# Re-ordering the input loads of a fused attention and FFN kernel over three DMA queues, with a new order of the small steps in its second block

## The chip, the cores and the metric

The kernel runs on one core of one Trainium2 chip. The metric is the device time of one execution in microseconds (us); smaller is better. Before the change the median of three executions was 339.74 us (338.42 to 339.96).

## The reference, cut to what matters

Eight batches of linear attention give `x`, and `x` goes through a gated feed-forward network (FFN). Batches, heads, tokens and head width are 8, 8, 576, 64; the FFN is 512 to 1536 to 512.

```python
def phi(x, c, s):                       # c, s: cosine and sine of the token's position
    r = np.maximum(x, 0.0)
    return np.concatenate([r * c, r * s], axis=-1)
q_p = phi(q, cos_w, sin_w);  k_p = phi(k, cos_w, sin_w)
kv  = np.einsum('bhsf,bhsd->bhfd', k_p, v);   z = np.sum(k_p, axis=2)
num = np.einsum('bhsf,bhfd->bhsd', q_p, kv)
den = np.einsum('bhsf,bhf->bhs', q_p, z)[..., None] + 1e-06
x   = num / den                          # then tokens x (heads*width) = 4608 x 512

xn  = x / np.sqrt(np.mean(x * x, -1, keepdims=True) + 1e-06) * rms_g
g   = xn @ w_gate;  out = (g / (1 + np.exp(-g)) * (xn @ w_val)) @ w_out
```

## The kernel before

The FFN runs in blocks of 512 tokens, one per batch. Block b has 16 steps. Steps 0 to 11 are gate and value matmuls (`psG`, `psV`), and steps 12 to 15 are output matmuls (`psC`). Between them sits the attention of batch b+1: the feature maps `k_phi` and `q_phi` (half on VectorE, half on ScalarE), the cast of v, the transposes of q, the k-z-v matmuls (`kv` and `z` of the reference), the numerator and denominator matmuls (`nd_pe`, below "numerator/denominator"), the norm, and the transpose of x that the next block multiplies. In block 0 the transposes run on TensorE; from block 1 on they are DMA transposes issued by SyncE. The last 64 tokens of a batch (the "tail") are handled in pairs of batches and make a ninth block.

A load is issued by an engine into a queue of DMA work, and lands some time later. All loads of q, k and v are issued by SyncE, in the order in which they are needed. The three weights are loaded by the GpSimd queue, which casts them to bf16 on the way.

```python
nc.scalar.preload_act_table(AF.Silu)
V, A, G = nc.vector, nc.scalar, nc.gpsimd
LOW, HIGH = (0, 4), (4, 8)                       # heads
# ... load_main, load_tail and load_pair call nc.sync.dma_start ...
load_main("k", k, 0, LOW, two)
load_main("k", k, 0, HIGH, two)
load_tail("k", k, 0)
load_pair("q", 0, 0)                             # two of the four token columns of q
load_main("v", v, 0, LOW)
first["v"] = load_tail("v", v, 0)
load_main("v", v, 0, (4, 6))
load_main("v", v, 0, (6, 8))
load_pair("q", 0, 1)
# ... the opening: attention of batch 0, and a third of block 0's first steps ...

def first_loads_of_1():
    d = load_main("k", k, 1, bufs=two)
    tc.add_manual_dep(d.ins, weight_dmas[4].ins.name, SYNC_DEP, reason="after the weights")
    load_tail("k", k, 1)
    gate = load_main("q", q, 1)
    load_main("v", v, 1, LOW)
    load_main("v", v, 1, HIGH)
    load_tail("v", v, 1)
    for i in range(4):
        d = nc.gpsimd.dma_start(out=wo[:, 3*i : 3*i+3, :], in_=moe_w_out[...])
        wo_dmas.append(d)
        if i == 0:
            tc.add_manual_dep(d.ins, gate.ins.name, SYNC_DEP, reason="after batch 1")
```

The last two lines are a gate: GpSimd does not start loading `w_out` until q of batch 1 has landed.

The order of the small steps in block 1 (`late` is true there, `nb` is batch 2; each step's DMA transposes follow its feature map):

```python
kb, kn = (b, (c + 1) // 2) if late else ...      # k_phi of batch 2, piece c
qn = 5 + (c * 3) // 5 if late else c             # q_phi and its DMA transpose, c = 0..4
vb, vn = (b, 3) if late else ...                 # cast of v
kz, nds = (7, (8, 10, 12, 13)) if late else ...  # k-z-v; numerator/denominator 0..3
# x_norm and the DMA transpose of x follow one step after each of nds
...
at(1, 2 + bb, "post", q_phi, ..., bb, 4, ...)    # tails of q, batches 0 and 1, steps 2 and 3
at(1, 2 + bb, "post", q_tr_dma, bb, 4)
at(1, 3, "post", load_tail, "q", q, 2)
at(1, 6, "pe", nd_pe, 1, 4, psA)                 # tail of the first pair of batches
at(1, 7, "post", x_tr_dma, 1, 4)
```

## Time and profile before

The profiled execution took 340.11 us, its span is 338.3 us and the mean granted TensorE clock is 0.988.

| landmark (profiled execution) | us |
|---|---|
| first FFN matmul | 19.91 |
| block 1 starts (first 256-column `psG` group) | 60.20 |
| step 2 of block 1 | 64.80 |
| block 2 starts | 101.98 |
| its second `psG` group | 105.17 |
| end of the span | 338.3 |

From the page of the kernel before, these are the busy times (share of the span, instruction count), the load of the DMA engines in 40 slices of 8.5 us (tenths) and the chain that ended last, by engine.

```profile
PE 322.0 (95%) x2157; PEld 163.9 (48%) x2193; DVE 181.5 (54%) x372; ACT 169.4 (50%) x327; POOL 38.1 (11%) x83
...
DMA  8999999948793966797769676967552220020014
...
PE 87%; DMA 4%; issue 2%; ACT 2%; DVE 2%; SPq 2%; POOL 0%; ACTq 0%; DVEq 0%; POOLq 0%
```

TensorE (PE) is the bound, but over the first eight slices, some 68 us, the DMA engines are full too.

The next lines are from the timeline of TensorE of the kernel before. The columns are start, length, engine, source line, operation, output from inputs, shape, count; the bracket gives the idle time before it and what ended it.

```profile
19.91 0.38 PE L511 MATMUL psG<-xnT,wg 128*128 128x128 bf16 x4 [0.30 <-DVE xnT L273]
...
44.63 0.39 PE L423 MATMUL psC<-wo,hT 128*128 128x512 bf16 x1 [0.59 <-DMA wo<-in_moe_w_out_dram]
...
74.14 0.60 PE L321 MATMUL psA<-kvzs,qtT 128*64 128x65 bf16 x15 [2.12 <-DMA qtT<-qp]
74.68 1.46 PE L403 MATMUL psG<-xnT,wg 128*128 128x512 bf16 x3
...
101.98 1.89 PE L403 MATMUL psG<-xnT,wg 128*128 128x512 bf16 x4 [2.54 <-DMA xnT<-xn]
...
105.17 1.03 PE L403 MATMUL psG<-xnT,wg 128*128 128x512 bf16 x4
```

TensorE stands still twice, in block 1 (until 74.14) and at its end (until 101.98), and works at half rate afterwards. A group of four 512-column matmuls takes 1.03 us in the last line, but 1.89 us just after the second wait. Both waits cost about 3.6 to 4 us each with that tail.

GpSimd's own waits in the same kernel show the gate at work:

```profile
POOL wo L601 <- DMA rq<-in_q_dram: 12.7, 1, 12.7
```

GpSimd waited 12.7 us, once, for q of batch 1 before it issued the load of `w_out`. GpSimd is no bottleneck, so this wait costs little by itself: TensorE's 0.59 us for `w_out` at 44.63.

### The profile page before, as it was taken

Reading aid. Unit: us, or ns where it says so; the run is one execution under the profiler, and the core shown is the slowest. Engines: PE = TensorE matmul, PEld = TensorE weight load, DVE = VectorE, ACT = ScalarE, POOL = GpSimd, SP = SyncE. Lnnn points to the kernel's source line nnn. Section 1 sums busy time; section 2 is a strip of 40 time slices with the busy share of each in tenths; the row PEclk is TensorE's granted clock in tenths of the full one; section 3 lists DMA queues with packets and bytes.
Section 4 is the critical chain, followed back from the end, with each engine's and each line's share of the span. In section 5 each row is a group of like instructions: output and inputs, shape, how many; then the busy total and the mean of one; then the engine's idle time right before and its main releaser. Section 6 shows DMA issues by size and latency. Waiting matters only on the chain.

```text
span 338.3 us, 5906 instructions
## 1 busy us (share of the span) xinstructions
PE 322.0 (95%) x2157; PEld 163.9 (48%) x2193; DVE 181.5 (54%) x372; ACT 169.4 (50%) x327; POOL 38.1 (11%) x83
## 2 busy tenths in 40 slices
PE   8889999879979999999999999999999999999994
PEld 3568455535433544454445444544454444444441
DVE  4675747575843576557536864685467323204410
ACT  5655844756454546554655465546645233223321
POOL 3520301101120012001100120011001100000000
PEclk9999999989997999999999999999999999999999
DMA  8999999948793966797769676967552220020014
GB/s 230 267 208 265 274 179 278 336 109 166 183 238 86 228 179 177 180 222 184 201 160 221 171 217 158 211 177 215 144 79 46 85 72 1 2 105 19 2 31 94
DMA packets 94957, 54.14 MB, mean 160 GB/s; under 512 B 59984, under 2 KB 90192, under 8 KB 94928
## 3 DMA queue, kind: packets, MB, share of 16 engines
q1 hardware_dynamic: 90160, 49.04, 57.6%
q0 software_dynamic: 4768, 4.72, 8.5%
q8 instruction: 17, 0.28, 0.4%
q14 instruction: 12, 0.10, 0.1%
HBM read 38.01 MB, written 9.44 MB: 140 GB/s over the span
## 4 chain that ended last, share of the span: by engine, by line
PE 87%; DMA 4%; issue 2%; ACT 2%; DVE 2%; SPq 2%; POOL 0%; ACTq 0%; DVEq 0%; POOLq 0%
PE psG L403 26%; PE psV L403 26%; PE psC L423 23%; PE psA L299 3%; PE psA L314 2%; DMA rv<-in_v_dram 2%; PE psG L423 1%; DMA xnT<-xn 1%; PE psO L511 1%; PE psG L511 1%; SPq L85 1%; PE psV L511 1%; DMA qtT<-qp 1%; SPq L76 1%; ACT scr L352 1%
## 5 line engine op out<-in xcount | busy, mean ns | idle before, releaser
L418 DVE TENSOR_TENSOR hT<-psV,sg 128x512 bf16<-128x512 f32 x102 | 70.3, 689 | 105.4 <-PE psV L403 78.8
L412 ACT ACTIVATE sg<-psG 128x512 f32<-128x512 f32 x102 | 60.6, 594 | 72.1 <-PE psG L403 67.0
L403 PE MATMUL psG<-xnT,wg 128*128 128x512 bf16 (+1 forms) x353 | 92.3, 379 | 4.5 <-DMA xnT<-xn 2.5
L403 PE MATMUL psV<-xnT,wv 128*128 128x512 bf16 (+1 forms) x364 | 93.3, 378 | 0.6 <-issue 0.2
L423 PE MATMUL psC<-wo,hT 128*128 128x512 bf16 x394 | 90.8, 379 | 1.2 <-DMA wo<-in_moe_w_out_dram 0.6
L403 PEld LDWEIGHTS <-wv 128*128 128x128 bf16 x416 | 41.1, 99 | 48.7 <-issue 2.2
L423 PEld LDWEIGHTS <-hT 128*128 128x128 bf16 x432 | 41.3, 98 | 48.3 <-DMA wo<-in_moe_w_out_dram 0.8
L403 PEld LDWEIGHTS <-wg 128*128 128x128 bf16 x416 | 38.9, 98 | 45.4 <-issue 3.0
L357 POOL TENSOR_TENSOR rs<-ms,mhalf 128x1 f32<-128x1 f32 x36 | 20.2, 562 | 206.0 <-ACT scr L352 206.0
L271 ACT COPY osb<-psC 128x512 f32<-128x512 f32 x33 | 19.4, 587 | 46.8 <-PE psC L423 46.8
L352 ACT ACTIVATE scr<-xt 128x513 bf16<-128x513 f32 x36 | 22.9, 636 | 24.8 <-DVE xt L340 23.9
L364 DVE SCALAR_TENSOR_TENSOR xn<-xt,rs,gb 128x512 bf16<-128x512 f32 x36 | 27.3, 760 | 14.1 <-POOL rs L357 13.9
L340 DVE TENSOR_TENSOR xt<-psA,rec 128x512 f32<-128x512 f32 x35 | 24.2, 691 | 1.2
L212 ACT ACTIVATE qp<-rq,tab 128x512 bf16<-128x512 f32 x32 | 22.2, 713 | 2.3 <-DMA rq<-in_q_dram 2.3
L212 ACT ACTIVATE kpm<-rk,tab 128x512 bf16<-128x512 f32 (+1 forms) x34 | 21.2, 675 | 2.5 <-DMA rk<-in_k_dram 2.4
L214 DVE TENSOR_SCALAR kpm<-rk,tab 128x512 bf16<-128x512 f32 (+1 forms) x38 | 15.2, 451 | 3.3 <-DMA rk<-in_k_dram 3.3
L314 PEld LDWEIGHTS <-qpT 128*128 128x128 bf16 x256 | 12.3, 98 | 8.0 <-issue 1.4
L214 DVE TENSOR_SCALAR qp<-rq,tab 128x512 bf16<-128x512 f32 x32 | 15.4, 493 | 0.6 <-DMA rq<-in_q_dram 0.6
L443 PE MATMUL psG<-warm 128*128 128x512 bf16 x47 | 13.8, 439 | 1.2 <-DVE fidx L149 1.2
L314 PE MATMUL psA<-kvzs,qpT 128*128 128x65 bf16 x248 | 13.0, 194 | 0.6 <-DVE xt L340 0.3
L403 PE MATMUL psG<-xnt_tail,wg 128*128 128x512 bf16 x48 | 12.3, 379 | 0.1
L403 PE MATMUL psV<-xnt_tail,wv 128*128 128x512 bf16 x47 | 12.1, 379 | 0.0
(82 smaller groups left out, 191.4 us busy)
## 6 DMA issues: line engine op xcount, KB each, us to landing
out_dram<-osb SPq DMA_DIRECT2D x32, 256.0 KB, 2.9
rv<-in_v_dram SPq DMA_DIRECT2D x22, 256.0 KB, 3.3
rk<-in_k_dram SPq DMA_DIRECT2D x20, 256.0 KB, 3.6
rq<-in_q_dram SPq DMA_DIRECT2D x20, 256.0 KB, 3.1
rk<-in_k_dram SPq DMA_DIRECT2D x2, 1024.0 KB, 7.0
rq<-in_q_dram SPq DMA_DIRECT2D x2, 1024.0 KB, 9.0
rv<-in_v_dram SPq DMA_DIRECT2D x3, 512.0 KB, 9.2
wo<-in_moe_w_out_dram POOLq DMA_DIRECT2D x4, 384.0 KB, 7.3
```

The lines of the kernel that those rows point to most:

```text
L212: nc.scalar.activation(out=out_ap, in_=in_ap, func=AF.Relu, scale=scale)
L214: eng.tensor_scalar(out=out_ap, in0=in_ap, scalar1=scale, scalar2=0.0, op0=ALU.mult, op1=ALU.max)
L271: nc.scalar.copy(out=o, in_=i)
L314: nc.tensor.matmul(o[:, g, i, :], lhsT=qpT[(b, 0)][:, h, j * P : (j + 1) * P], rhs=kvzs[b][:, g, i * E : (i + 1) * E], start=True, stop=True,)
L340: nc.vector.tensor_tensor(out=xt[:, 0:DM].rearrange("p (b h d) -> p b h d", b=2, d=D), in0=o[:, :, :, 0:D], in1=rec[:, :, :].unsqueeze(3). ...
L352: nc.scalar.activation(out=scr[:, :], in_=xt[:, 0 : DM + 1], func=AF.Square, scale=1.0 / math.sqrt(DM), accum_out=ms[:, :],)
L357: nc.gpsimd.tensor_tensor(out=rs[:, :], in0=ms[:, :], in1=mhalf[:, :], op=ALU.pow)
L364: nc.vector.scalar_tensor_tensor(out=xn[:, :], in0=x_of[(b, j)][:, 0:DM], scalar=rs_of[(b, j)][:, :], in1=gb[:, :], op0=ALU.mult, op1=ALU. ...
L403: nc.tensor.matmul(pst[bank][:, cols[0] : cols[1]], lhsT=w[:, t, n * P : (n + 1) * P], rhs=x[:, t, cols[0] : cols[1]], start=(t == 0), sto ...
L412: nc.scalar.activation(out=sg[:, :], in_=psG[bank][:, :], func=AF.Silu)
L418: nc.vector.tensor_tensor(out=hTs[blk][:, n, :], in0=psV[bank][:, :], in1=sg[:, :], op=ALU.mult)
L423: nc.tensor.matmul(bank, lhsT=hTs[blk][:, n, j * P : (j + 1) * P], rhs=wo[:, n, :], start=(n == 0), stop=(n == NNT - 1),)
```

## The change

It has four parts, named (a) to (d) as in the prediction:

- (a) The opening loads are split over SyncE's and ScalarE's queues, so that they are issued sooner. The load of ScalarE's activation table moves behind ScalarE's issues. Also, the first k-z-v uses single banks of PSUM (the memory into which TensorE writes), so that one half can be evicted while the other is computed.
- (b) v of batch 1 goes to the GpSimd queue, and the gate on `w_out` goes.
- (c) The tail of the first pair moves from step 6 of block 1 to step 14, to end the first wait. The rest of batch 2's attention moves up to one step earlier.
- (d) With that, the last transpose of x comes one step earlier, to end the second wait.

```diff
 first = {}
+load_pair("q", 0, 0, A)                 # A: ScalarE's queue
 load_main("k", k, 0, LOW, two)
+load_main("v", v, 0, LOW, queue=A)
 load_main("k", k, 0, HIGH, two)
+first["v"] = load_tail("v", v, 0, A)
 load_tail("k", k, 0)
-load_pair("q", 0, 0)
-load_main("v", v, 0, LOW)
-first["v"] = load_tail("v", v, 0)
+load_main("v", v, 0, (6, 8), queue=A)
 load_main("v", v, 0, (4, 6))
-load_main("v", v, 0, (6, 8))
 load_pair("q", 0, 1)
+nc.scalar.preload_act_table(AF.Silu)    # was the first instruction
 # ... cut: kvzs as one tile per bank, kvz_half in psG[1] and psV[1], more buffers ...
 x_norm(0, 1)
+load_main("v", v, 1, LOW, queue=G)      # G: GpSimd's queue
+load_main("v", v, 1, HIGH, queue=G)
+load_tail("v", v, 1, G)
 # ...
-gate = load_main("q", q, 1)
-load_main("v", v, 1, LOW)
-load_main("v", v, 1, HIGH)
-load_tail("v", v, 1)
+load_main("q", q, 1)
 # ... in the loop over the four pieces of w_out:
-    if i == 0:
-        tc.add_manual_dep(d.ins, gate.ins.name, SYNC_DEP, reason="after batch 1")
 # ... block 1:
-qn = 5 + (c * 3) // 5 if late else c
+qn = 4 + (c * 3) // 5 if late else c
-kz, nds = (7, (8, 10, 12, 13)) if late else (4, (5, 7, 9, 11))
+kz, nds = (6, (7, 9, 11, 12)) if late else (4, (5, 7, 9, 11))
-at(1, 6, "pe", nd_pe, 1, 4, psA)        # and its post, norm and transpose at 6 and 7
+at(1, 14, "pe", nd_pe, 1, 4, psA)       # now at 14 and 15
```

More of the change, by code (lines that the diff above doesn't have):

```diff
@@ L61 @@
     psO = ps_open.tile([P, 2, 512], FP32, name="psO")
-    nc.scalar.preload_act_table(AF.Silu)
     V, A, G = nc.vector, nc.scalar, nc.gpsimd
@@ L69, with load_main @@
     raw = {}
-    def load_main(which, src, b, heads=(0, 8), bufs=one):
+    def load_main(which, src, b, heads=(0, 8), bufs=one, queue=nc.sync):
         key = (which, b)
@@ L75, in load_main @@
         h0, h1 = heads
-        return nc.sync.dma_start(
+        return queue.dma_start(
             out=raw[key][:, h0:h1, :],
@@ L79, in load_main, with load_tail @@
         )
-    def load_tail(which, src, b):
+    def load_tail(which, src, b, queue=nc.sync):
         t = two.tile([P, 4, D], FP32, name=f"r{which}t", tag=f"r{which}t")
@@ L84, in load_tail @@
         for g in range(2):
-            d = nc.sync.dma_start(
+            d = queue.dma_start(
                 out=t[64 * g : 64 * g + 64, :, :],
@@ L104, in load, with load_pair @@
         last_load[(which, b)] = load_tail(which, src_of[which], b)
-    def load_pair(which, b, jj):
+    def load_pair(which, b, jj, queue=nc.sync):
         key = (which, b)
@@ L111, in load_pair @@
         view = src_of[which][b, :, 0:512, :].rearrange("h (p j) d -> p h j d", j=4)
-        return nc.sync.dma_start(
+        return queue.dma_start(
             out=raw[key][:, :, jj * 2 * D : (jj + 1) * 2 * D],
@@ L245, in q_dst @@
         if (b, c // 4) not in qpT:
-            qpT[(b, c // 4)] = two.tile(
+            qpT[(b, c // 4)] = (two if c < 4 else four).tile(
                 [P, H, 512] if c < 4 else [P, 4, P], BF16,
@@ L303, in kvz_evac, with kvz_half, kvz_half_evac @@
     def kvz_evac(eng, b, pst, bank):
-        if b not in kvzs:
-            kvzs[b] = two.tile([P, 2, 4 * E], BF16, name="kvzs", tag="kvzs")
-        copy(eng, kvzs[b][:, bank, :], pst[:, bank, 0 : 4 * E])
+        kvzs[(b, bank)] = three.tile([P, 4 * E], BF16, name="kvzs", tag=f"kvzs{bank}")
+        copy(eng, kvzs[(b, bank)][:, :], pst[:, bank, 0 : 4 * E])
+    def kvz_half(b, view, heads):
+        o = view[:, 0, 0 : 4 * E].rearrange("p (h e) -> p h e", e=E)
+        for h in heads:
+            for c in range(5):
+                lhsT = kp_main[b][:, c, h, :] if c < 4 else kpt[b % 2][:, h % 4, :]
+                rhs = vvm[b % 2][:, c, h, :] if c < 4 else vvt[b % 2][:, h, :]
+                nc.tensor.matmul(
+                    o[:, h % 4, :], lhsT=lhsT, rhs=rhs, start=(c == 0), stop=(c == 4)
+                )
+    def kvz_half_evac(eng, b, view, bank):
+        kvzs[(b, bank)] = three.tile([P, 4 * E], BF16, name="kvzs", tag=f"kvzs{bank}")
+        copy(eng, kvzs[(b, bank)][:, :], view[:, 0, 0 : 4 * E])
     def nd_pe(b, j, pst):
@@ L315, in nd_pe @@
                     o[:, g, i, :], lhsT=qpT[(b, 0)][:, h, j * P : (j + 1) * P],
-                    rhs=kvzs[b][:, g, i * E : (i + 1) * E], start=True, stop=True,
+                    rhs=kvzs[(b, g)][:, i * E : (i + 1) * E], start=True, stop=True,
                 )
@@ L323, in nd_pe @@
                         lhsT=qpT[(bb, 1)][:, i, 64 * g : 64 * g + 64],
-                        rhs=kvzs[bb][:, g, i * E : (i + 1) * E], start=True, stop=True,
+                        rhs=kvzs[(bb, g)][:, i * E : (i + 1) * E], start=True, stop=True,
                     )
@@ L477 @@
     filler(2, idle)
-    kvz_pe(0, psA, range(0, 4))
+    half_view = {
+        g: t[:, :].rearrange("p (b c) -> p b c", b=1) for g, t in ((0, psG[1]), (1, psV[1]))
+    }
+    kvz_half(0, half_view[0], range(0, 4))
     filler(1, idle)
@@ L482 @@
     v_cast(A, 0, (7, 8))
-    kvz_evac(A, 0, psA, 0)
-    kvz_pe(0, psA, range(4, 6))
+    kvz_half(0, half_view[1], range(4, 6))
     filler(1, idle)
-    kvz_pe(0, psA, range(6, 8))
+    kvz_half(0, half_view[1], range(6, 8))
     filler(2, idle)
-    kvz_evac(V, 0, psA, 1)
+    kvz_half_evac(A, 0, half_view[0], 0)
+    kvz_half_evac(V, 0, half_view[1], 1)
     for c in (2, 3):
@@ L738 @@
     at(1, 3, "post", load_tail, "q", q, 2)
-    at(1, 6, "pe", nd_pe, 1, 4, psA)
-    at(1, 6, "pre", nd_post, 1, 4, psA)
-    at(1, 6, "post", x_sq, 1, 4)
-    at(1, 7, "post", x_norm, 1, 4)
-    at(1, 7, "post", x_tr_dma, 1, 4)
+    at(1, 14, "pe", nd_pe, 1, 4, psA)
+    at(1, 14, "pre", nd_post, 1, 4, psA)
+    at(1, 14, "post", x_sq, 1, 4)
+    at(1, 15, "post", x_norm, 1, 4)
+    at(1, 15, "post", x_tr_dma, 1, 4)
     for blk in range(1, 9):
```

## The prediction

> **What bounds the kernel now.** The profile page has PE busy 95% of 338.3 us; the chain of waits is PE for 87%. Outside a saturated middle, the chain leaves PE in four places.
> 1. Opening: the chain runs SyncE's load issues, the v load (lands 12.77), ACT cast, k-z-v, numerator/denominator from 15.10, first FFN matmul at 19.91.
> 2. About 43.6 to 45.1: transposes and a wait for w_out; PE idle 0.59 us.
> 3. Block 1, step 6: PE waits 2.12 us at 72 to 74.14 for the transposed q tails (L321). The next eight 512-column matmuls take 3.2 us instead of 1.73 (cold clock): about 3.6 us in all.
> 4. End of block 1: PE waits 2.54 us (to 101.98) for the last x transpose of batch 2, and is cold again: about 4.0 us.
>
> **What changes.**
> (a) Opening. Five load issues move from SyncE to ACT, ahead of the table load (1.28 us). I expect this to lose. The Trainium skill ("DMA: Bandwidth & Descriptors", Queues, rings and completion order) says all queues share 16 engines, which go round-robin by packet; this trace agrees on saturation: the DMA row reads 9 from about 2.3 us on. So bytes do not come faster, only in another order: q (512-byte rows) now shares with k. In the instruction order ACT's fifth issue (v, heads 6 and 7) waits for the completion of its first (q)[...], and the table load, sine table and every k_phi on both engines stand behind it. Before, k landed at 4.65 and 6.35, about 310 GB/s. Against the whole of k, q should land at about 7 to 7.5 (estimate); adding 0.55 issue, 1.28 table, 0.3 sine, phi starts at 9 to 9.7 instead of 4.7. From there the vector engine's k phi (3.2), q phi (0.9), two q copies and v casts give numerator/denominator at 17.5 to 18.5. The 26 fillers end at 9.3, so PE idles about 3 us and is cold for the first k-z-v. Single banks save only about 0.3 us (PE waited 0.25 us for an eviction). Net +3.2 us (range -0.5 to +4.5).
> (b) v of batch 1 on GpSimd, w_out not gated by q: removes the w_out wait and brings batch 2's loads earlier: -0.8 us. PE is full there, so little else.
> (c) Tail of the first pair at step 14: removes stall 3. But k-z-v and numerator/denominator move one step earlier. SyncE still issues, in order, tail transposes (69.2, 71.2), two q tail loads (to 73.75), and only then batch 2's first q transpose, landing 3.4 us later (about 77.2). PE now wants it at about 75: a new stall near 2 us with the same cold period, plus up to 0.6 us at k-z-v behind the v cast. Net 0.
> (d) The last x transpose is issued one output step earlier (2.6 us), which covers stall 4: -3.9 us.
>
> **Sum:** 339.7 + 3.2 - 0.8 + 0 - 3.9 = **338.2 us**, 80% range 334.5 to 342. Chances: faster by over 2% 0.06, within 2% 0.91, slower by over 2% 0.03.
>
> **What would show it.** (a) first ACTIVATE on k near 9 us, ACT's v issue delayed to q's landing, first FFN matmul at 22 to 24 us. (b) no w_out wait near 45 us. (c) no L321 wait; a wait of numerator/denominator on qpT at step 7, followed by 379-to-634 ns matmuls at half rate. (d) no xnT wait between block 1 and block 2.
>
> **What would make it wrong.** If q lands near 5 us, or phi is not held by ACT's queue, the opening gains about 1 us and the total is near 334. If the q transpose comes in time, another 3 us go. If the x transpose is still late behind GpSimd's 1/rms or stores, stall 4 stays and the result is slower than before.

## More of the kernel before

Last, the DMA view of the kernel before, from 26 to 43.4 us, when batch 1 and `w_out` are loaded: queues with packets, MB and share, then loads with the issuing queue, count, KB each and the median time from issue to landing. Queue q1 is SyncE's, q0 is GpSimd's, whose weights are counted after the cast to bf16.

```profile
DMA packets 5384, 4.65 MB, mean 267 GB/s; under 512 B 1451, under 2 KB 5380, under 8 KB 5380
q1 hardware_dynamic: 4496, 3.47, 69.8%
q0 software_dynamic: 884, 1.12, 37.6%
...
rk<-in_k_dram SPq DMA_DIRECT2D x1, 1024.0 KB, 7.6
rq<-in_q_dram SPq DMA_DIRECT2D x1, 1024.0 KB, 8.8
```

k of batch 1 lands 7.6 us after its issue and q 8.8 us after.

## The result and the profile after

The changed kernel took 350.23 us, the median of four executions (348.62 to 352.58), against 339.37 us for the kernel before (four executions). The ratio is 1.0328, with a 95% interval of 1.0264 to 1.0393: slower. A ratio here is the mean time of one kernel's fast runs over that of the other's of the same rounds, so it is not quite the ratio of the medians quoted. The prediction of 338.2 us, with a range that ended at 342, was wrong.

The profiled execution is the slowest of the four, 352.58 us (span 350.8 us, clock 0.977). Its page has these lines, in the same places as above:

```profile
PE 327.7 (93%) x2193; PEld 165.9 (47%) x2193; DVE 180.8 (52%) x372; ACT 169.5 (48%) x327; POOL 40.7 (12%) x87
...
DMA  8999995645767896779677766986571320020013
...
PE 78%; DMA 11%; ACT 4%; DVE 3%; issue 2%; ACTq 0%; POOL 0%; DVEq 0%
```

The DMA share of the chain rose from 4% to 11%. One link in the list of that chain (start, length, what) holds most of it:

```profile
32.41 20.30 DMA rq<-in_q_dram
```

That is the load of q of batch 1, issued at 32.41 and landed 20.3 us later. The timeline of TensorE of the kernel after shows what it did:

```profile
23.61 0.38 PE L527 MATMUL psG<-xnT,wg 128*128 128x128 bf16 x4 [0.37 <-DVE xnT L273]
...
45.95 1.02 PE L416 MATMUL psG<-xnT,wg 128*128 128x512 bf16 x4 [2.56 <-ACT sg L425]
...
53.52 0.62 PE L262 MATMUL psA<-ident,qp 128*128 128x128 bf16 x8 [3.71 <-ACT qp L212]
55.33 1.01 PE L262 MATMUL psV<-ident,qp 128*128 128x128 bf16 x8 [1.20 <-DVE hT L431]
56.14 1.06 PE L436 MATMUL psC<-wo,hT 128*128 128x512 bf16 x2
...
61.26 0.60 PE L436 MATMUL psC<-wo,hT 128*128 128x512 bf16 x2
...
92.03 0.62 PE L327 MATMUL psA<-kvzs,qpT 128*128 128x65 bf16 x8 [2.57 <-DMA qpT<-qp]
92.46 1.90 PE L416 MATMUL psG<-xnT,wg 128*128 128x512 bf16 x4
...
115.35 1.02 PE L416 MATMUL psG<-xnT,wg 128*128 128x512 bf16 x4 [0.28 <-DMA xnT<-xn]
```

Between 43 and 56 us TensorE idles three times, and then works at half rate: two matmuls take 1.06 us at 56.14 and 0.60 us at 61.26. The first idle time is put down to ScalarE's silu (`sg`). ScalarE's timeline says why the silu was late:

```profile
43.47 1.95 ACT L212 ACTIVATE kpm<-rk,tab 128x512 bf16<-128x512 f32 x3 [3.77 <-DMA rk<-in_k_dram]
...
52.74 1.33 ACT L212 ACTIVATE qp<-rq,tab 128x512 bf16<-128x512 f32 x2 [4.88 <-DMA rq<-in_q_dram]
```

ScalarE works in order. It stood 3.77 us before the feature map of k and 4.88 us before that of q, and the silus behind them stood with it. The DMA view of the kernel after, over the same 26 to 43.4 us, shows where the loads were:

```profile
DMA packets 3430, 4.34 MB, mean 250 GB/s; under 512 B 462, under 2 KB 3140, under 8 KB 3428
q0 software_dynamic: 2069, 3.19, 86.4%
q1 hardware_dynamic: 1359, 1.13, 27.3%
...
rk<-in_k_dram SPq DMA_DIRECT2D x1, 1024.0 KB, 15.1
rq<-in_q_dram SPq DMA_DIRECT2D x1, 1024.0 KB, 20.3
```

The engines moved about the same (4.34 MB for 4.65), but the queues have changed places. SyncE's queue, with k and q, moved 1.13 MB instead of 3.47. GpSimd's, with v and `w_out`, moved 3.19 MB instead of 1.12. k took twice as long to land, and q more than twice. While both queues had work, they took turns. From 35 to 40 us the same view has:

```profile
q0 software_dynamic: 586, 0.61, 70.5%
q1 hardware_dynamic: 585, 0.60, 44.7%
```

The packets are equal to within one, so k and q got every second packet.

The ledger of the two profiled executions, by the landmarks (after minus before, us). The changed kernel starts block 1 at 74.18 us, its step 2 at 78.77 and the second `psG` group of block 2 at 117.07.

| stretch | before | after | difference | predicted |
|---|---|---|---|---|
| up to the first FFN matmul (a) | 19.91 | 23.61 | +3.7 | +3.2 |
| from there to the start of block 1 (b) | 40.29 | 50.57 | +10.3 | -0.8 |
| step 2 of block 1 to the second `psG` group of block 2 (c, d) | 40.37 | 38.30 | -2.1 | -3.9 |
| all the rest | | | +0.6 | 0 |
| sum | 338.3 | 350.8 | +12.5 | -1.5 |

"All the rest" is the 4.6 us before step 2 of block 1, which are alike, and what follows block 2's second group (233.13 and 233.73 us). The profiled execution is the slowest of its kernel, so the sum is larger than the 10.9 us between the medians.

### The profile page after: what moved, and what is told of

Same layout as the page of the kernel before. It is cut to its first block, busy times and chain, and to the rows that moved or that the text cites. A ratio compares the mean times of both kernels' runs of the same rounds, so it can differ in the third digit from the quotient of the medians.

```text
span 350.8 us, 5948 instructions
## 1 busy us (share of the span) xinstructions
PE 327.7 (93%) x2193; PEld 165.9 (47%) x2193; DVE 180.8 (52%) x372; ACT 169.5 (48%) x327; POOL 40.7 (12%) x87
## 4 chain that ended last, share of the span: by engine, by line
PE 78%; DMA 11%; ACT 4%; DVE 3%; issue 2%; ACTq 0%; POOL 0%; DVEq 0%
PE psC L436 23%; PE psG L416 22%; PE psV L416 22%; DMA rq<-in_q_dram 7%; PE psA L327 2%; PE psA L299 2%; PE psG L436 1%; DMA xnT<-xn 1%; ACT kpm L212 1%; PE psG L456 1%; DVE xt L353 1%; DMA out_dram<-osb 1%; DMA qpT<-qp 1%; PE psV L262 1%; ACT scr L365 1%
## 5 line engine op out<-in xcount | busy, mean ns | idle before, releaser
L416 PE MATMUL psG<-xnT,wg 128*128 128x512 bf16 (+1 forms) x368 | 93.5, 377 | 4.3 <-ACT sg L425 2.6
L436 PE MATMUL psC<-wo,hT 128*128 128x512 bf16 x408 | 92.9, 382 | 0.0
L456 PE MATMUL psG<-warm 128*128 128x512 bf16 x49 | 15.7, 470 | 1.2 <-DVE fidx L149 1.2
## 6 DMA issues: line engine op xcount, KB each, us to landing
wo<-in_moe_w_out_dram POOLq DMA_DIRECT2D x4, 384.0 KB, 14.3
```

The lines of the kernel that those rows point to most:

```text
L416: nc.tensor.matmul(pst[bank][:, cols[0] : cols[1]], lhsT=w[:, t, n * P : (n + 1) * P], rhs=x[:, t, cols[0] : cols[1]], start=(t == 0), sto ...
L436: nc.tensor.matmul(bank, lhsT=hTs[blk][:, n, j * P : (j + 1) * P], rhs=wo[:, n, :], start=(n == 0), stop=(n == NNT - 1),)
```

## The experiments

There are eleven kernels in three sets (no e6 is on record), each set on one chip with its own runs of the kernel before. All gave correct results.

### First set: which half of part (b) delays batch 1

Two theories stood against each other. Theory G: the removed gate lets `w_out` compete with k and q. Theory V: v on the GpSimd queue takes the engines before k and q are served. The third kernel undoes both; the fourth keeps (b) and undoes only the opening. The kernel before took 339.48 us here (338.92 to 340.24, 7 runs).

**e1_gate**: the changed kernel with the gate put back.

```diff
-load_main("q", q, 1)
+gate = load_main("q", q, 1)
     wo_dmas.append(d)
+    if i == 0:
+        tc.add_manual_dep(d.ins, gate.ins.name, SYNC_DEP, reason="after batch 1")
```

> The changed kernel with one thing undone: the first w_out load waits again until q of batch 1 has landed; v of batch 1 stays on the GpSimd queue. Theory G (the removed gate lets w_out compete with k and q of batch 1): q lands near 42 us instead of 52.7, the first FFN matmul of block 1 starts near 64 to 65 us instead of 74.2, and the total is 340 to 343 us. Rival V (v on the GpSimd queue is what starves k and q): q still lands after 50 us and the total stays at 348 or more.

**e2_v_sp**: the changed kernel with v of batch 1 back on SyncE, and no gate.

```diff
 x_norm(0, 1)
-load_main("v", v, 1, LOW, queue=G); load_main("v", v, 1, HIGH, queue=G); load_tail("v", v, 1, G)
 load_main("q", q, 1)
+load_main("v", v, 1, LOW); load_main("v", v, 1, HIGH); load_tail("v", v, 1)
```

> The changed kernel with the other thing undone: v of batch 1 comes again behind q on the SyncE queue; w_out stays without its gate. Theory G: w_out still takes its share beside k and q, and v now comes last of all, so the wait moves to q or v and the total stays at 348 to 352. Rival V: the total falls to 340 to 343.

**e3_gate_v_sp**: both of these edits.

```diff
 # the edits of e1_gate and of e2_v_sp, both
```

> Both undone. Both theories: k, q, v and w_out come as in the kernel before, block 1 starts 3.5 to 4 us later than in the kernel before (64 instead of 60.2, the loss in the opening), block 1 wins 2 us, total 340 to 342. If v on GpSimd is harmless, this equals the run with the gate alone within 1 us.

**e4_open_old**: the changed kernel, with the opening loads and the table load as before.

```diff
+nc.scalar.preload_act_table(AF.Silu)     # first again
-load_pair("q", 0, 0, A)                  # and the other opening loads likewise:
+load_main("k", k, 0, LOW, two)           # k, k tail, q, v, all on SyncE
```

> The changed kernel with the opening loads as before (one queue, table load first). If the loss of the opening adds to that of the late q: first FFN matmul at 19.5 to 20, total down by 3.7 to 346.5. Rival, that the moment at which q lands sets the end of block 0 whatever PE did earlier: first FFN matmul at 19.5 to 20 all the same, q still lands at 51 to 53, block 1 still starts near 73, and the total stays within 1.5 us of 350.2.

Measured (the middle columns are from the profiled execution, us; the median and range are of fast runs):

| kernel | k lands after | q lands after | block 0, first FFN matmul to block 1 | median (range) | ratio to before, 95% |
|---|---|---|---|---|---|
| before | 7.6 | 8.8 | 40.29 | 339.48 | |
| after (first comparison) | 15.1 | 20.3 | 50.57 | 350.23 | 1.0328 (1.0264 to 1.0393) |
| e1_gate | 11.6 | 10.8 | 39.91 | 341.95 (340.89 to 343.16) | 1.0071 (1.0034 to 1.0108) |
| e2_v_sp | 7.6 | 13.0 | 40.21 | 343.90 (343.20 to 345.76) | 1.0191 (1.0127 to 1.0254) |
| e3_gate_v_sp | 8.3 | 9.5 | 39.51 | 340.38 (338.77 to 342.21) | 1.0025 (0.9981 to 1.0070) |
| e4_open_old | 14.3 | 20.2 | 50.66 | 347.35 (346.28 to 349.51) | 1.0237 (1.0197 to 1.0277) |

For e2_v_sp the ratio is not one of fast runs: it equals the mean of the last three executions, the slow one among them, over the mean of the kernel before. The three fast ones give 1.014.

The DMA view of e1_gate over 26 to 43.4 us, to set beside the two above:

```profile
q1 hardware_dynamic: 2896, 2.29, 51.0%
q0 software_dynamic: 1011, 2.14, 50.1%
...
rk<-in_k_dram SPq DMA_DIRECT2D x1, 1024.0 KB, 11.6
rq<-in_q_dram SPq DMA_DIRECT2D x1, 1024.0 KB, 10.8
```

And that of e2_v_sp:

```profile
rk<-in_k_dram SPq DMA_DIRECT2D x1, 1024.0 KB, 7.6
rq<-in_q_dram SPq DMA_DIRECT2D x1, 1024.0 KB, 13.0
```

With v on GpSimd and the gate in place, k lands late (11.6 instead of 7.6); with v on SyncE and no gate, q does (13.0 instead of 8.8). Together they make 15.1 and 20.3. v on GpSimd is also issued earlier, at 22.94 us in the kernel after, ahead of k at 28.36, where the kernel before issued it behind q, at 30.32. No run separates the queue from the time of issue.

Neither theory alone holds, because the parts do not add: in medians, restoring only the gate gains 8.3 us, restoring only v gains 6.3, and restoring both gains 9.9. By the expectations, e1_gate came into theory G's range, e2_v_sp into neither, and e3_gate_v_sp into its own.

In the profiled executions either delay alone leaves block 0 as short as before. But this rests on the longer opening, which these kernels keep. The kernel before had q on chip by 38.6 us (issue at 29.75 plus 8.8), and ScalarE began its feature map at 39.71: 1.2 us of room. In e1_gate and in e2_v_sp q landed at 43.5 us, and the feature map began at 44.47 and 45.00 without a wait, because the first FFN matmul stood at 24.67 and 25.20 instead of 19.91. With the old opening the same landing would have come almost 4 us too late (an estimate: 43.5 against 39.71); no run tests one half of (b) with it. With both delays q landed at 52.7 us, past any such room, and the price is the 7.5 us of idle time and the half-rate stretch that the timeline of the kernel after shows.

One thing stays open. e2_v_sp was profiled in its fastest execution (343.20 us), and where the slower ones lost time is not seen. In the profile v itself was late there: VectorE waited 2.31 us for it, and TensorE waited 0.69 us soon after.

e4_open_old gains 2.9 us over the changed kernel in the medians, for an opening that is 4.35 us shorter in the profiles; this lies between its two expectations, nearer to that of losses that add. Block 0 is as long as in the changed kernel: its TensorE waits 4.53 us for the silu behind k, and q lands 1.8 us earlier (50.9 for 52.7 us). So block 1 starts 4.3 us earlier (69.92 for 74.18). Some 1.3 us of that is lost again in block 1 and at its end, where the waits for the transposed q and for the last transpose of x are 3.32 and 0.79 us instead of 2.57 and 0.28.

### Second set: what costs 3.7 us in the opening, and which order block 1 wants

The prediction blamed ScalarE. Its fifth issue waits for its first load (q), and the table load stands behind it. ScalarE's timeline in the kernel after agrees:

```profile
6.75 0.38 ACTq L75 DMA_DIRECT2D rv<-in_v_dram  x1
7.16 1.28 ACT L126 ACT_TABLE_LOAD   x1 [7.16 <-DMA rq<-in_q_dram]
...
8.70 2.50 ACT L212 ACTIVATE kpm<-rk,tab 128x256 bf16<-128x256 f32 x6
```

The same lines of the kernel before come down to one, with the feature map of k four microseconds earlier:

```profile
4.68 2.63 ACT L212 ACTIVATE kpm<-rk,tab 128x256 bf16<-128x256 f32 x6 [2.44 <-DMA rk<-in_k_dram]
```

A trace that agrees with a theory does not yet show that it limits. Theory A: ScalarE's blocked queue is the cause. Theory B: q and v share the engines with k, so k itself comes late, and ScalarE's wait only coincides with that. The kernel before took 339.11 us here (337.23 to 340.75, 11 runs).

**e5_act_free**: e3_gate_v_sp, with the table load right after ScalarE's first four issues and the fifth moved to SyncE, so that ScalarE waits for nothing.

```diff
-load_main("v", v, 0, (6, 8), queue=A)
+nc.scalar.preload_act_table(AF.Silu)
 load_main("v", v, 0, (4, 6))
+load_main("v", v, 0, (6, 8))
 load_pair("q", 0, 1)
-nc.scalar.preload_act_table(AF.Silu)
```

> The kernel with gate and v restored (340.4 us), with the opening loads still split over two queues, but nothing blocks ACT: its fifth load (v, heads 6 and 7) goes to SyncE, and the table load follows its four remaining issues. Theory A (the loss in the opening is ACT standing behind a wait for q): sine table near 5 us, first k phi near 5.3 when k lands, first FFN matmul at 19.3 to 20.5 instead of 23.7, total 336 to 337.5. Rival B (sharing the DMA engines makes k or v late, whatever ACT does): first FFN matmul still at 22 or later, total 339 or more.

It took 340.56 us (338.53 to 342.74, 6 runs), ratio 1.0040 (1.0002 to 1.0079); e3_gate_v_sp had 340.38 against its own runs of before. ScalarE's timeline in e5_act_free:

```profile
5.39 1.71 ACT L212 ACTIVATE kpm<-rk,tab 128x256 bf16<-128x256 f32 x4 [0.31 <-DMA rk<-in_k_dram]
9.12 0.91 ACT L212 ACTIVATE kpm<-rk,tab 128x256 bf16<-128x256 f32 x2 [2.02 <-DMA rk<-in_k_dram]
10.95 0.51 ACT L212 ACTIVATE kpt<-rkt,tab 128x256 bf16<-128x256 f32 x1 [0.92 <-DMA rkt<-in_k_dram]
```

The first feature map came at 5.39 instead of 8.70 us. But the second half of k landed only at 9.12 and its tail at 10.95. In the kernel before, VectorE began on the second half at 6.40. The first FFN matmul is at 23.45 (e3_gate_v_sp: 23.66). So theory A is not the whole cause: with ScalarE free, the loss stays, because k is late, as theory B says. But the traces do not clear ScalarE. In e3_gate_v_sp the chain up to the first FFN matmul runs through ScalarE's wait for q and the table load, and VectorE ends the feature map of k's tail at 11.80 us. In e5_act_free it runs through the load of k's tail, and the same map ends at 11.31 (8.33 in the kernel before). The two limits lie side by side, and either alone would cost most of the loss. That is an estimate from these times: no run has an early k and a blocked ScalarE. The profiles of kernels with a split opening that has q and v beside k put the first FFN matmul between 23.45 and 25.20, so that 0.2 us is also within their spread.

**e7_banks_sched**: all loads as before; only the single banks and the changed order of block 1 are kept.

```diff
 # against e4_open_old: the edits of e1_gate and of e2_v_sp, both
+    tc.add_manual_dep(d.ins, gate.ins.name, SYNC_DEP, reason="after batch 1")
-load_main("v", v, 1, LOW, queue=G)       # and the other two
+load_main("v", v, 1, LOW)                # and the other two, after q
```

> The kernel before with only the single banks and the new order of block 1 (all loads as before). First FFN matmul near 19.3; a wait of about 3 us for the transposed q in block 1, no wait of more than 1 us for the last x transpose; about 2 us won in block 1. Total 336 to 337.5. If the single banks win nothing in the opening, 337.5 or more.

It took 336.20 us (335.03 to 338.52, 6 runs), ratio 0.9926 (0.9886 to 0.9966). The first FFN matmul is at 19.22 us, 0.7 earlier than before, which is what the single banks give. The changed order keeps one large wait, in TensorE's timeline of e7_banks_sched:

```profile
78.96 0.43 PE L328 MATMUL psA<-kvzs,qpT 128*128 128x65 bf16 x8 [3.62 <-DMA qpT<-qp]
```

This is the wait that the prediction named for part (c). Its reason was SyncE's order of issues, in which q tail loads go ahead of q's transposes. SyncE's timeline of the kernel after has them so:

```profile
87.24 1.28 SPq L84 DMA_DIRECT2D rqt<-in_q_dram  x2
88.68 2.63 SPq L254 DMA_TRANSPOSE qpT<-qp  x2
```

**e8_mid_sched**: e7_banks_sched with another order in block 1, meant to keep (d) and lose that wait.

```diff
-qn = 4 + (c * 3) // 5 if late else c
+qn = (4, 4, 5, 5, 8)[c] if late else c
-kz, nds = (6, (7, 9, 11, 12)) if late else ...
+kz, nds = (7, (8, 10, 11, 12)) if late else ...
-at(1, 3, "post", load_tail, "q", q, 2)
+at(1, 4, "post", load_tail, "q", q, 2)        # after q's first transposes
```

> As the run with the single banks and the new order, but with the order of block 1 mended: k-z-v of batch 2 at step 7 as before, numerator and denominator at 8, 10, 11 and 12, q phi at step 4 as in the change, and the two q tail loads queued on SyncE after the first two q transposes instead of ahead of them. If the wait for the transposed q comes from SyncE's order and the cold clock behind it costs as much as before: the wait falls below 0.7 us, no matmul there runs at half rate, both stalls of block 1 are gone, total 331.5 to 333.5. If the transposes are late for another reason: the wait stays over 2 us and the total over 335.

It took 335.78 us (332.95 to 337.03, 6 runs), ratio 0.9884 (0.9841 to 0.9927). TensorE's timeline of e8_mid_sched:

```profile
76.92 0.43 PE L328 MATMUL psA<-kvzs,qpT 128*128 128x65 bf16 x8 [0.32 <-DMA qpT<-qp]
...
84.98 0.53 PE L328 MATMUL psA<-kvzs,qpT 128*128 128x65 bf16 x8 [2.20 <-DVE xt L354]
```

The wait for q's transpose fell from 3.62 to 0.32 us; k-z-v and the first numerator/denominator also stand one step later here, so the load order and that step share the credit. But a new wait of 2.20 us came up at 84.98. ScalarE's timeline gives its source:

```profile
80.90 0.51 ACT L213 ACTIVATE qp<-rqt,tab 128x256 bf16<-128x256 f32 x1 [2.06 <-DMA rqt<-in_q_dram]
```

The tail's load was now issued later, its feature map at step 8 waited for it on both engines, and the eviction `xt` on VectorE stood behind. My edit had moved a wait, not removed it, and the total missed the expected 331.5 to 333.5.

**e9_free_mid**: the order of e8_mid_sched with the opening of e5_act_free. It asks whether the split opening is worth anything once block 0 and block 1 do not hide it.

```diff
 # the order edits of e8_mid_sched on top of e5_act_free
```

> The mended order of block 1 and the split opening that does not block ACT together. If splitting the issue gains bandwidth or latency, it beats the mended order with the old opening by 0.5 us or more; if it only spares issue time that nobody waited for, the two are within 1 us (331 to 334).

It took 339.52 us (336.18 to 340.96, 6 runs), ratio 0.9999 (0.9954 to 1.0043), with the first FFN matmul at 23.48. Beside e8_mid_sched (19.35), the opening split in this way is 4.1 us longer, and in the medians 3.7 us of that reach the end.

### Third set: mending what the second showed

The kernel before took 338.17 us here (337.49 to 340.44, 11 runs).

**e10_mended**: e8_mid_sched, with the feature map of the q tail at step 10 instead of 8.

```diff
-qn = (4, 4, 5, 5, 8)[c] if late else c
+qn = (4, 4, 5, 5, 10)[c] if late else c
```

> The mended order of block 1 with the old opening, with one more correction: the q tail's phi moves from step 8 to step 10, because its load landed only at 80.9 us and held ACT and the silu behind it, which became a wait of 2.20 us before numerator and denominator. If that is the whole cause: waits of at most 0.7 us remain in block 1, no matmul at half rate there, the second FFN step of block 2 starts near 98 instead of 101.5, and the total falls another 3 to 3.5 us to 332 to 333. If the wait comes from numerator and denominator standing at 10, 11 and 12 in a row, it stays near 2 us and the total at 335 to 336.

It took 334.24 us (333.48 to 334.62, 6 runs), ratio 0.9872 (0.9842 to 0.9902), the best. It beats the kernel before by 1.3% with an interval clear of 1. The waits in block 1 fell as expected; the total missed the expected 332 to 333. Its interval overlaps those of e7_banks_sched and e8_mid_sched, so the totals do not rank the three orders; the waits in the traces do. TensorE's timeline of e10_mended has the waits that are left in block 1 and at its end (a third, of 0.57 us, is left out):

```profile
76.84 0.43 PE L328 MATMUL psA<-kvzs,qpT 128*128 128x65 bf16 x8 [0.52 <-DMA qpT<-qp]
...
97.56 1.02 PE L417 MATMUL psG<-xnT,wg 128*128 128x512 bf16 x4 [1.04 <-DMA xnT<-xn]
```

None is followed by half-rate matmuls.

**e11_k_first**: e3_gate_v_sp, with a second queue in the opening, but for k alone. SyncE issues the first half of k, ScalarE only the second half and then the table load; the rest is on SyncE in the order of before.

```diff
 load_main("k", k, 0, LOW, two)
+load_main("k", k, 0, HIGH, two, queue=A)
+nc.scalar.preload_act_table(AF.Silu)
 load_tail("k", k, 0)
 load_pair("q", 0, 0)                      # this and all that follows on SyncE
```

> The kernel with gate and v restored and the changed order of block 1 (340.4 us), with an opening that uses both queues, but only for the two halves of k; q, v and the tails follow on SyncE in the order of the kernel before. If the loss in the opening comes from what shares the DMA engines with k (q and v) and not from the use of a second queue: both halves of k land by 6.5 us, k tail by 8, the first FFN matmul starts at 19 to 20, total 336 to 337.5. If a second queue as such costs: first FFN matmul at 22 or later, total 339 or more.

It took 337.05 us (335.85 to 337.45, 6 runs), ratio 0.9952 (0.9920 to 0.9983). The timeline of ScalarE of e11_k_first:

```profile
5.65 2.50 ACT L212 ACTIVATE kpm<-rk,tab 128x256 bf16<-128x256 f32 x6 [2.90 <-DMA rk<-in_k_dram]
```

All six pieces of k run here in one go, and the first FFN matmul is at 19.13 us, against 23.66 in e3_gate_v_sp. So the second queue did no harm by itself. ScalarE waits for no issue here, and in e5_act_free it did not either; what differs between the two is what shares the engines with k. With ScalarE free, then, what harmed was that q and v, needed later, shared the engines with k.

**e12_best**: the order of e10_mended with the opening of e11_k_first.

```diff
 # the order edits of e10_mended on top of e11_k_first
```

> The corrected order of block 1 and the opening with the two halves of k on two queues. If the halves on two queues gain latency, it beats the old opening by 0.5 us or more; otherwise within 1 us of it, 332 to 333.5.

It took 335.81 us (333.36 to 337.28, 6 runs), ratio 0.9915 (0.9871 to 0.9960). The first FFN matmul is at 19.23, so this opening is as good as the old one and no better. In TensorE's timeline of e12_best the transpose of x came later than in e10_mended:

```profile
99.11 1.02 PE L416 MATMUL psG<-xnT,wg 128*128 128x512 bf16 x4 [2.54 <-DMA xnT<-xn]
```

SyncE issued the last one at 94.95 us (e10_mended: 94.08), and it took 4.12 us to land (3.43). Why is not settled. The total missed the expected 332 to 333.5, and its interval overlaps that of e10_mended.

## Why the prediction was wrong

The step that failed is (b): "removes the w_out wait and brings batch 2's loads earlier: -0.8 us. PE is full there, so little else." The wait for `w_out` did go (0.59 us before, none after), but the stretch grew by 10.3 us. I had costed what the removed gate was waiting for and not what it protected. "PE is full there" was true of the kernel before because of that gate and of SyncE's single queue. I had the means to see it: the DMA row read 9 in that stretch, GpSimd's waits showed it held for 12.7 us by q, and I had myself used the rule that applies. The Trainium skill ("DMA: Bandwidth & Descriptors", "Queues, rings and completion order") says that a DMA engine goes round-robin over the queues that have work, packet by packet. From 35 to 40 us the two queues moved 586 and 585 packets, and q landed after 20.3 us instead of 8.8. I applied it to the opening and not to the next load phase. The first set shows the cause by taking it away: with gate and v restored, block 0 is 39.51 us long and the whole kernel is level with before (1.0025), its longer opening made up for by the shorter block 1.

Point by point for the rest:

- **(a) The size was right and the path was there, but I missed a second limit beside it.** Predicted +3.2, measured +3.7 (net of about -0.7 from the single banks, predicted -0.3). The steps I named happened: ScalarE's fifth issue waited for q until 6.75 us, the table came at 7.16 and the first feature map at 8.70. Yet taking all that away (e5_act_free) moved the first FFN matmul by only 0.2 us. The second half of k, at 9.12 us, and its tail, at 10.95, came almost as late as the path that I had named, and putting k first with ScalarE free (e11_k_first) took the loss away. I had the bytes "in another order" in the text, but followed only the late table to the end. The same page of the Trainium skill, "Issuing engines are not separate DMA queues", says that issuing on several engines saves only the sequencers' issue time, usually small beside the DMA. Over the first 14 us the kernel before moved 3.60 MB and the one after 3.63.
- **(c) The new wait was foreseen; its balance was too kind.** The numerator/denominator waits 2.57 us for the transposed q, with half-rate matmuls after it (four in 1.90 us), as predicted. My reading of the two traces puts (c) at about +1.6 (1.5 and some rounding), where I had put 0: before lost 2.12 us idle and about 1.4 at half rate, and after lost 2.57 idle, about 1.4 at half rate, and 0.52 and 0.60 in two smaller waits (for the v cast and for an eviction). This is one execution of each: in e3_gate_v_sp, with the same order of block 1, the wait of 3.11 us was not followed by half-rate matmuls, and the stretch of the ledger took 36.79 us instead of 38.30.
- **(d) was right.** The wait at the start of block 2 fell from 2.54 us with half-rate matmuls to 0.28 without: about -3.7, predicted -3.9. With (c) at +1.6 that makes the measured -2.1.
- **What I said would make it wrong.** I named q landing early, the transposes coming in time and the last transpose staying late. None of them was it. The failed step was the one to which I had given the least thought, because it looked small.

The halves of the change are of opposite sign. Without the changes to the loads, the rest of it is worth -0.7% (e7_banks_sched), and with the order mended -1.3% (e10_mended).

## What to carry to other kernels

While the DMA engines were full, a second queue added no bandwidth in this kernel (3.60 and 3.63 MB in the first 14 us); it only changed whose bytes went first. So order loads by when they are needed, and before removing a gate or moving a load, ask what it will compete with, not only who waits for it. A delay that looks free may be using room that another loss has made, so test such edits together as well as alone, and ask where the room comes from. And a wait that agrees with a theory need not be the only limit: take it away and see whether the end moves.

## What the Trainium skill lacked or had wrong

- "DMA: Bandwidth & Descriptors", "Queues, rings and completion order", has the round-robin between queues, but not how much it can cost one load. Here k landed after 15.1 us instead of 7.6 and q after 20.3 instead of 8.8, at nearly the same total rate (250 and 267 GB/s, weights counted after the cast).
- The same page, "Issuing engines are not separate DMA queues", says that little is saved by several issuing engines. It does not say that this can lose: 3.7 us in the medians with q and v on ScalarE's queue beside k (e9_free_mid against e8_mid_sched), while with only half of k there the opening lost nothing (first FFN matmul at 19.13 us in e11_k_first, 19.22 in e7_banks_sched).
- No page that I read warns that a later issue can wait for the landing of an earlier load. In the kernel after, ScalarE's fifth issue was held until 6.75 us, when its load of q had landed. In e5_act_free ScalarE no longer waits, and SyncE's next load of v was held 3.5 us, until 6.77 us, for that same load of q on ScalarE's queue. In both programs the held issue is the ninth load and q is the first, so the wait seems to go with the place in the program. The rule behind it is not shown; no run isolated it.
- "TensorE: Matmul & The Clock Gate", "Part 1: The HAM clock gate", says the clock falls after at least one idle window of about 3.4 us, with windows that run freely. Idle gaps of 2.12 and 2.54 us (before) and 2.57 (after, at 92.03) were followed by half-rate matmuls here, while 2.56 us (after, at 45.95), 2.54 us (e12_best, at 99.11) and 3.11 us (e3_gate_v_sp, at 81.57) were not. So a gap below 3.4 us was not safe here, and its length alone did not decide; free-running windows would fit that, but no run here tests it.
